# Side by side in the first expert too: its values and residuals from the fifth step on

## The chip, the cores and the metric

The kernel runs on one core of one Trainium2 chip. The metric is the device time in microseconds; lower is better. A core has five engines with a program each: TensorE for matmuls (PE in the profile, with its weight loads as PEld), VectorE (DVE), ScalarE (ACT), GpSimd (POOL) and SyncE (SP), which here issues most of the DMAs.

## The reference

The output is a gated mix of two parts for 2048 tokens of width 448: a Fourier mix of the tokens (part a) and a mixture of 8 experts (part b), in which each token goes to the two experts with the largest gate.

```python
gates = _softmax(xt @ wg, axis=-1)
topk_idx = jnp.argsort(-gates, -1)[:, :K]              # K = 2 of E = 8
...
h = _gelu(jnp.einsum("nd,edf->nef", xt, w1))           # 448 -> 1792
y = jnp.einsum("nef,efd->ned", h, w2)                  # 1792 -> 448
out = jnp.einsum("ne,ned->nd", cw, y)
...
return g * a + (1 - g) * b
```

The change touches the first product of one expert, `x @ w1` with the gelu behind it.

## The kernel before

**Stages.** The first 36 us hold the Fourier part's hidden transform, its quarter-length sequence transform and the gate logits. Then come the 8 experts, which the kernel orders by how many tokens they drew. Expert 0 (the fullest) has room for 552 tokens, experts 1 to 3 for 544, 528 and 528, experts 4 to 7 for 496 (`CAPS`). Each expert takes `NF` = 14 steps, one for each 128 of the 1792 hidden units, so there are 112 steps; below, step u of expert 0 is its step number, 0 to 13, and step 14 is the first of expert 1.

**One step.** `up(u)` forms 128 hidden units for all tokens of the expert in PSUM, and `down(u)` multiplies the result with 128 rows of `w2` into five PSUM banks that collect over the 14 steps. To keep precision, every operand is a rounded value and the residual that the rounding left: `hi` and `lo` of the weights, and in the tile `X[e]` four chunks of 128 features of rounded tokens (index 0 to 3) and three of residuals (4 to 6; the residual of the short fourth chunk sits in that chunk's free rows). A product is the sum of value times value, value times residual, and residual times value.

The tokens of a step are worked in two parts (`hf` 0 and 1), as a PSUM bank (the tile `acc`, three buffers) takes 512 columns of 4 bytes. In expert 0 the parts are 276 and 276 columns. Each part is 11 matmuls into one `acc`: `hi` with three value chunks, `hi` with three residual chunks, `hi` with the fourth chunk, `lo` with four value chunks. Then ScalarE applies the gelu from PSUM to the tile `g` (L794).

In experts 1 to 3 `pairs(e)` is true: the first part is 256 columns, and one matmul of 512 columns streams a value chunk and its residual chunk side by side, into the two halves of the bank. That part is 8 matmuls, and its sum has to be finished: ScalarE copies the residual half from PSUM to `g` (L792), VectorE adds the value half to it (L793), and then ScalarE applies the gelu to `g` in place (L794).

After both parts, `g` is rounded to `gh`, by ScalarE in experts 1 to 3 and in steps 4 to 13 of expert 0 (L805), else by VectorE (L807), and VectorE forms the residual `gl` (L811) and some small pieces (L818, L819). `down(u)` needs `gh` and `gl`.

**Order.** The order of instructions on TensorE, VectorE, ScalarE and SyncE is that of the program text. The loop over u issues: `turn_due` (a tile of gathered tokens of the next expert is split into values, L695 on ScalarE, and residuals, L696 and L697 on VectorE); `prep(u + 2)` (the weights of the step after next are rounded on ScalarE, L226, and their residuals formed on VectorE, L231, after which SyncE fetches further weights); while u < 11 `advance(2)`, the next pieces of the routing work; `stage` (VectorE transposes a gathered tile, `blocks`, L684, and GpSimd gathers another, L675); `up(u + 1)`; `down(u)`; and `side_work`, a check of the transform matrices on VectorE. In experts 1 to 3 the side work is issued between the two parts of `up`, in expert 0 behind `down`; it begins at u = 11.

**Routing work in expert 0.** The routing generator makes the token lists and weights on VectorE with long instructions: `oa` (L394), `ob` and `vtok` (L398, L402), `piece` (L420, 16 short ones), `part` and `vw` (L426 to L433), then the place tables. TensorE multiplies in between (L407 into `acc`, whose result gives `tok`, from L410; L438 into `acc`, whose result gives `wgt`, from L441). GpSimd gathers the tokens of expert 1 by `piece` from step 6 on, in five tiles of up to 128 tokens, with two buffers for gathered tiles (`xg`).

Of the kernel before, what the change touches and what calls it, by code (L numbers as in the profile page):

```python
# [20 lines left out]
P = 128  # L21
# [5 lines left out]
E = 8  # L27
F = 1792
NF = F // P
CAPS = (552, 544, 528, 528, 496, 496, 496, 496)  # L30
CMAX = 576
FULL = 4
# [33 lines left out]
def r32(ap):  # L66
    return ap.bitcast(F32)
# [7 lines left out]
def tile_kernel(ctx: ExitStack, tc: tile.TileContext, xt, xrows, xplain, wg, whid, cq, cw, cspec, edge, refs, wquad, whall, cgen, wcat, out):  # L75
# [103 lines left out]
    def clear(i):  # L179
        if i == 0:  # L180
            rt["zero"] = mp.tile([P, D], F32, name="yt", bufs=2)
            ve.memset(rt["zero"], 0.0)
        if i < NT + NCT:
            sp.dma_start(out[i * P : (i + 1) * P, :], rt["zero"])
# [9 lines left out]
    jobs = [(e, f) for e in range(E) for f in range(NF)]  # L194
# [18 lines left out]
    def extra(e):  # L213
        return max(0, CAPS[e] - FULL * P)

    def apart(e):
        return 0 < extra(e) <= Q
# [19 lines left out]
    def prep(k):  # L237
        if k < len(jobs):
            upper(k)
            lower(k)  # L240
# [250 lines left out]
    def advance(n=1):  # L491
        for _ in range(n):
            next(route, None)
# [205 lines left out]
    def turn0(c, n):  # L699
        if c == 0:  # L700
            X[0] = xp.tile([P, 2 * NC - 1, CMAX], F32R, name="X")
        pt = (psy if c > 1 else ps).tile([P, NC, P], F32, name=f"y{c - 2}" if c > 1 else "acc")
        xg = XG.pop(c)
        for k in range(NC):
            te.transpose(pt[:, k, :n], xg[:n, k * P : (k + 1) * P], ident[:n, :n])
        sl = slice(c * P, c * P + n)
        se.activation(X[0][:, :NC, sl], pt[:, :, :n], AF.Copy)
        TU[c] = pt, sl, n
# [3 lines left out]
    def left0(c):  # L712
        pt, sl, n = TU.pop(c)
        ve.tensor_tensor(X[0][:, NC:, sl], pt[:, : NC - 1, :n], r32(X[0][:, : NC - 1, sl]), OP.subtract)
        ve.tensor_tensor(X[0][64:P, NC - 1, sl], pt[64:P, NC - 1, :n], r32(X[0][64:P, NC - 1, sl]), OP.subtract)
# [5 lines left out]
    def turn_due(e, step, lag, pace):  # L721
        c = due(e, step - lag - 1, pace)
        if c is not None:
            turn(e, c)

    def stage(e, step, lag, pace):
        c = due(e, step - lag, pace)
        if c is not None:
            blocks(e, c)
        c = due(e, step, pace)  # L730
        if c is not None:
            gather(e, c)
# [24 lines left out]
    UP, GH, Y, REST = 0, {}, {}, {}  # L757
    last = len(jobs) - 1

    def pairs(e):  # L760
        return e > 0 and CAPS[e] > FULL * P

    def up(u, between=lambda: None):
        e, f = jobs[u]
        hi, lo = W[u]
        cap = CAPS[e]
        rem = extra(e)
        span = FULL * P if broad(u) else cap
        g = mp.tile([P, CMAX], F32, name="g")
        nh = 1 if cap <= 512 else 2  # L770
        cut = 2 * P if u == 0 or pairs(e) else cap // nh
        for hf in range(nh):
            cs = slice(hf * cut, cap if hf == nh - 1 else cut)
            xs = slice(cs.start, span if hf == nh - 1 else cut)
            n = cs.stop - cs.start
            acc = ps.tile([P, 512], F32, name="acc")
            part = lambda w, x, c: (w[:, c * P : (c + 1) * P], X[e][:, x + c, xs], xs.stop - xs.start)
            both = pairs(e) and hf == 0
            if both:
                steps = [(hi[:, c * P : (c + 1) * P], X[e][:, c : c + NC + 1 : NC, cs], 2 * n) for c in range(NC - 1)]  # L780
            else:
                steps = [part(hi, 0, c) for c in range(NC - 1)] + [part(hi, NC, c) for c in range(NC - 1)]
            steps += [part(hi, 0, NC - 1)] + [part(lo, 0, c) for c in range(NC)]
            if u == 0 and hf == 1:
                steps = steps[: NC - 1] + steps[2 * NC - 1 : -1] + steps[NC - 1 : 2 * NC - 1] + steps[-1:]
            for s, (a, b, m) in enumerate(steps):
                te.matmul(acc[:, :m], a, b, start=s == 0, stop=s == len(steps) - 1)  # L787
                if u == hf == 0 and s in (2, 5):
                    turn0(s // 3 + 3, tl0[s // 3 + 3])
                    left0(s // 3 + 3)  # L790
            if both:
                se.activation(g[:, cs], acc[:, n : 2 * n], AF.Copy)  # L792
                ve.tensor_tensor(g[:, cs], acc[:, :n], g[:, cs], OP.add)  # L793
            se.activation(g[:, cs], g[:, cs] if both else acc[:, :n], AF.Gelu_apprx_tanh)  # L794
            if hf == 0:
                between()
        if u == last:
            gh, gl = (stream.tile([P, DX], F32R, name=n) for n in ("hi", "lo"))
        else:
            gh = mp.tile([P, CMAX + RMAX], F32R, name="gh", bufs=3)  # L800
            gl = mp.tile([P, FULL * P], F32R, name="gl", bufs=3)
        main = cap - rem
        top = main if apart(e) else cap
        if pairs(e) or snug(e) and e < E - 1 or e == 0 and f >= 4:
            se.activation(gh[:, :top], g[:, :top], AF.Copy)  # L805
        else:
            ve.tensor_copy(gh[:, :top], g[:, :top])  # L807
        GH[u] = (gh, gl)

        def rests():  # L810
            ve.tensor_tensor(gl[:, :main], g[:, :main], r32(gh[:, :main]), OP.subtract)  # L811
            if apart(e):
                if f in LOTS:
                    rt["rest"] = mp.tile([P, NF, Q], F32, name="rest", bufs=2)
                REST[u] = rt["rest"][:, f - max(b for b in LOTS if b <= f)]
                ve.tensor_copy(REST[u][:, :rem], g[:, main:cap])
            elif rem:
                ve.memset(r32(gh[:, cap : main + RMAX]), 0.0)  # L818
                ve.tensor_tensor(gh[:, main + RMAX : main + RMAX + rem], g[:, main:cap], r32(gh[:, main:cap]), OP.subtract)  # L819

        if f == 0 and e > 0:
            return rests
        rests()

    def snug(e):
        return CAPS[e] == FULL * P - 16

    def broad(u):
        e, f = jobs[u]
        return snug(e) and (f < 2 and not snug(e - 1) or f == NF // 2 - 1 and e == E - 2)  # L830
# [266 lines left out]
    def side_work(s):  # L1097
# [27 lines left out]
        if s > end + 1 and 1 <= f < (NF - 3 if e == E - 1 else NF - 1) and len(summed) < NT:  # L1125
            mix(len(summed))

    up(UP, lambda: advance(2))
    def jump_hint():
        PE = mybir.EngineType.PE  # L1130
        tc.mark_branch_hint_location("rare", "LikelyTaken", [PE])
        mark = next(i for i in reversed(nc.cur_bb.bb.instructions) if i.engine == PE)
        tc.keep_in_program_order(SimpleNamespace(ins=mark))

    for u in range(UP, last):
        e, f = jobs[u]
        plan = (e + 1, f - 1, 2, 2) if e else (1, f - 6, 2, 1)
        turn_due(*plan)
        prep(u + 2)
        if u < UP + SIDE:  # L1140
            advance(2)
            clear(2 * (u - UP))
            clear(2 * (u - UP) + 1)
        if u == last - NF - 1:
            tc.keep_in_program_order(gp.drain())
        if u == UP + SIDE:
            for _ in route:
                pass
            ck = late.enter_context(tc.tile_pool(name="ck", bufs=2, side="right"))
        stage(*plan)  # L1150
        split = pairs(jobs[u + 1][0])
        if u + 3 == last:
            jump_hint()
        rests = up(u + 1, lambda: side_work(u - UP) if split else None)
        if u < last - 3:
            down(u, behind=rests)
        if not split:
            side_work(u - UP)
# [66 lines left out]
    with tc.For_i(0, n_a) as j:  # L1225
# [3 lines left out]
        for h in range(2):  # L1229
            hf = full.tile([P, 2 * D], F32, name="hf")  # L1230
# [133 lines left out]
```

## Time and profile before

| | |
|---|---|
| median of 3 runs | 620.47 us (620.4 to 620.85) |
| the profiled execution, its own time | 620.74 us |
| its span in the profile | 619.1 us |
| TensorE busy | 611.8 us, 99% of the span |
| VectorE busy | 482.8 us, 78% |
| ScalarE busy | 321.1 us, 52% |
| mean granted clock of TensorE | 0.997 |

The span runs from the first to the last instruction of the profiled execution; 1.6 us of its time lie outside. Busy times of matmuls are modelled, so the spacing of their starts says more than their durations.

### The profile page before, as it was taken

The page shows a single profiled execution, that of the slowest core. Times are in us where ns is not written, and L with a number is a line of the kernel's source. Part 1 is how long each engine was busy: PE and PEld are TensorE (multiplying, and loading weights), DVE is VectorE, ACT ScalarE, POOL GpSimd, SP SyncE. Part 2 cuts the span into 40 slices and gives each one's busy share as a digit, 9 for nine tenths or more (in the row PEclk, how much of TensorE's full clock was granted, in tenths as well). Part 3 has the DMA queues.
Part 4 walks back from the last instruction along what each step waited for, and adds up shares of the span by engine and source line. Part 5 has one row for each costly group of instructions (what it writes and reads, how often), then busy time and mean ns, then how long its engine had stood idle before and what let it go on. Part 6 is the DMA issues. An engine that isn't in the chain of part 4 may idle for free. (4 is left out here: it accounts for less than half of the span.)

```text
span 619.1 us, 10867 instructions
## 1 busy us (share of the span) xinstructions
PE 611.8 (99%) x3581; PEld 547.6 (88%) x3581; DVE 482.8 (78%) x1234; ACT 321.1 (52%) x642; POOL 219.8 (36%) x200
## 2 busy tenths in 40 slices
PE   9999999999999999999999999999999999999996
PEld 6999999999998999989999788888888888888885
DVE  8889688579978889879896698787995677566652
ACT  2553344566565566655565645554454545654440
POOL 2210075635154262444460445333350442142123
PEclk9999999999999999999999999999999999999998
DMA  8556455597667777777776868779576736768743
GB/s 345 188 160 216 158 190 166 145 257 236 214 226 190 207 239 235 237 190 209 242 235 224 200 201 264 237 208 285 191 241 195 154 117 146 158 149 181 148 84 76
DMA packets 58653, 122.94 MB, mean 199 GB/s; under 512 B 8356, under 2 KB 31740, under 8 KB 58592
## 3 DMA queue, kind: packets, MB, share of 16 engines
q1 hardware_dynamic: 47376, 101.95, 50.4%
q0 software_dynamic: 11072, 20.19, 17.5%
q8 instruction: 29, 0.48, 0.3%
q14 instruction: 32, 0.26, 0.1%
q10 hardware_dynamic: 144, 0.07, 0.0%
HBM read 106.27 MB, written 15.90 MB: 197 GB/s over the span
## 5 line engine op out<-in xcount | busy, mean ns | idle before, releaser
L861 PE MATMUL y<-ud,gh 128*128 128x448 f32 (+3 forms) x916 | 258.6, 363 | 0.0
L787 PE MATMUL acc<-X,hi 128*128 128x496 f32 (+5 forms) x1050 | 211.1, 337 | 0.0
L675 POOL DMA_INDIRECT xg<-xrows,piece x115 | 129.5, 1126 | 199.7 <-DVE xq L684 125.8
L787 PEld LDWEIGHTS acc<-X,hi 128*128 128x128 f32 x1050 | 171.8, 188 | 18.0 <-issue 1.1
L861 PEld LDWEIGHTS y<-ud,gh 128*128 128x128 f32 (+1 forms) x916 | 166.5, 185 | 12.7
L861 PE MATMUL y<-ud,gl 128*128 128x448 f32 (+1 forms) x444 | 162.3, 365 | 0.0
L794 ACT ACTIVATE g<-acc 128x496 f32<-128x496 f32 (+4 forms) x126 | 60.6, 481 | 166.1 <-PE acc L787 148.9
L787 PE MATMUL acc<-X,lo 128*128 128x496 f32 (+5 forms) x672 | 132.5, 319 | 0.0
L811 DVE TENSOR_TENSOR gl<-g,gh 128x512 fp32r<-128x512 f32 (+1 forms) x111 | 75.5, 680 | 62.8 <-ACT gh L805 61.5
L787 PEld LDWEIGHTS acc<-X,lo 128*128 128x128 f32 x672 | 104.8, 188 | 9.0
L926 POOL DMA_INDIRECT out<-ys,tok x36 | 64.3, 1787 | 109.4 <-DVE ys L916 35.1
L861 PEld LDWEIGHTS y<-ud,gl 128*128 128x128 f32 (+1 forms) x444 | 82.6, 186 | 11.7 <-DVE gl L811 0.2
L967 DVE CUSTOM_DVE_ANT_0 junk<-quads 128x512 f32<-128x512 f32 x128 | 87.8, 686 | 2.3
L231 DVE TENSOR_TENSOR lo<-raw,hi 128x512 fp32r<-128x512 f32 x112 | 77.0, 688 | 3.5 <-ACT hi L226 2.5
L226 ACT ACTIVATE hi<-raw 128x512 fp32r<-128x512 f32 x112 | 69.1, 617 | 0.0
L231 DVE TENSOR_TENSOR ud<-row,ud 128x448 fp32r<-128x448 f32 x112 | 69.1, 617 | 0.0
L226 ACT ACTIVATE ud<-row 128x448 fp32r<-128x448 f32 x112 | 63.1, 563 | 0.0
L805 ACT ACTIVATE gh<-g 128x512 fp32r<-128x512 f32 (+2 forms) x94 | 59.2, 630 | 3.0
L792 ACT ACTIVATE g<-acc 128x256 f32<-128x256 f32 x42 | 16.1, 382 | 42.9 <-PE acc L787 42.6
L794 ACT ACTIVATE g<-g 128x256 f32<-128x256 f32 x42 | 17.6, 418 | 39.4 <-DVE g L793 39.4
L1091 POOL DMA_DIRECT2D out<-ot x16 | 14.1, 904 | 57.0 <-ACT ot L1090 47.1
L793 DVE TENSOR_TENSOR g<-acc,g 128x256 f32<-128x256 f32 x42 | 17.3, 412 | 12.4 <-ACT g L792 12.4
(272 smaller groups left out, 386.0 us busy)
## 6 DMA issues: line engine op xcount, KB each, us to landing
quads<-cq SPq DMA_DIRECT2D x64, 512.0 KB, 5.2
raw<-wcat SPq DMA_DIRECT2D x112, 256.0 KB, 2.9
row<-wcat SPq DMA_DIRECT2D x112, 224.0 KB, 3.3
out<-yt SPq DMA_DIRECT2D x21, 224.0 KB, 3.3
xraw<-xt SPq DMA_DIRECT2D x8, 512.0 KB, 6.5
out<-ot POOLq DMA_DIRECT2D x16, 224.0 KB, 3.7
cw<-cw SPq DMA_DIRECT2D x4, 512.0 KB, 9.9
xg<-xrows,piece POOLq DMA_INDIRECT x115, 3.8
```

Source lines behind the costliest of these rows:

```text
L226: se.activation(hi[:, : raw.shape[-1]], raw, AF.Copy)
L231: ve.tensor_tensor(lo[:, :n], raw, r32(hi[:, :n]), OP.subtract)
L675: st = gp.indirect_dma_start(out=xg[:, q], out_offset=None, in_=xrows, in_offset=bass.IndirectOffsetOnAxis(ap=rt["piece"][:, e, g : g + 1] ...
L787: te.matmul(acc[:, :m], a, b, start=s == 0, stop=s == len(steps) - 1)
L792: se.activation(g[:, cs], acc[:, n : 2 * n], AF.Copy)
L793: ve.tensor_tensor(g[:, cs], acc[:, :n], g[:, cs], OP.add)
L794: se.activation(g[:, cs], g[:, cs] if both else acc[:, :n], AF.Gelu_apprx_tanh)
L805: se.activation(gh[:, :top], g[:, :top], AF.Copy)
L811: ve.tensor_tensor(gl[:, :main], g[:, :main], r32(gh[:, :main]), OP.subtract)
L861: te.matmul(Y[c][:m, o], a, b, start=f == 0 and s == 0, stop=f == NF - 1 and s == len(steps) - 1)
L926: st = gp.indirect_dma_start(out=out, out_offset=bass.IndirectOffsetOnAxis(ap=rt["tok"][:n, e, c : c + 1], axis=0), in_=ys[:n], in_offset= ...
L967: ve.tensor_tensor_reduce(out=junk[:, :512], in0=row(a[0])[:, a[1] * 512 : a[1] * 512 + 512], in1=row(b[0])[:, b[1] * 512 : b[1] * 512 + 5 ...
```

## The change

`pairs` gets the step as a second argument and becomes true for expert 0 from step 4 on as well. In these ten steps the first part of `up` is 256 columns with 8 matmuls (three of 512 columns, five of 256), followed by ScalarE's copy, VectorE's add and the gelu in place; the second part is 296 columns with 11 matmuls. Who rounds `g` to `gh` stays as it was, and the place of the side work too. Nothing else differs.

```diff
-    def pairs(e):
-        return e > 0 and CAPS[e] > FULL * P
+    def pairs(e, f=NF):
+        return CAPS[e] > FULL * P and (e > 0 or f >= 4)
...
-        cut = 2 * P if u == 0 or pairs(e) else cap // nh
+        cut = 2 * P if u == 0 or pairs(e, f) else cap // nh
...
-            both = pairs(e) and hf == 0
+            both = pairs(e, f) and hf == 0
...
-        if pairs(e) or snug(e) and e < E - 1 or e == 0 and f >= 4:
+        if pairs(e, f) or snug(e) and e < E - 1:
...
-        split = pairs(jobs[u + 1][0])
+        split = pairs(*jobs[u + 1]) and jobs[u + 1][0] > 0
```

## Rows read from the trace of the kernel before

**Rows 1.** The head of the page: the span, and each engine's busy time, share and instructions.

```profile
span 619.1 us, 10867 instructions
...
PE 611.8 (99%) x3581; PEld 547.6 (88%) x3581; DVE 482.8 (78%) x1234; ACT 321.1 (52%) x642; POOL 219.8 (36%) x200
```

**Rows 2.** The timeline of TensorE in expert 0 and the first two steps of expert 1; columns: start in us, us, engine, line, operation, out<-in, shape, count. In step 4 the first part begins at 56.87, the second at 58.26, `down` at 59.65. Then the two list products, the second part of step 12, both parts of step 14, and step 15.

```profile
56.87 1.04 PE L787 MATMUL acc<-X,hi 128*128 128x276 f32 x7
...
58.26 1.04 PE L787 MATMUL acc<-X,hi 128*128 128x276 f32 x7
...
59.65 0.57 PE L861 MATMUL y<-ud,gh 128*128 128x448 f32 x2
...
68.14 0.98 PE L407 MATMUL acc<-vtok,oa 128*128 128x40 f16 x32
...
91.61 1.86 PE L438 MATMUL acc<-vw,oa 128*128 128x120 bf16 x32
...
106.02 1.04 PE L787 MATMUL acc<-X,hi 128*128 128x276 f32 x7
...
115.90 0.98 PE L787 MATMUL acc<-X,hi 128*128 128x512 f32 x4
...
117.19 1.09 PE L787 MATMUL acc<-X,hi 128*128 128x288 f32 x7
...
121.52 0.97 PE L787 MATMUL acc<-X,hi 128*128 128x512 f32 x4
...
122.80 1.09 PE L787 MATMUL acc<-X,hi 128*128 128x288 f32 x7
...
124.26 0.56 PE L861 MATMUL y<-ud,gh 128*128 128x448 f32 x2
```

**Rows 3.** The timeline of VectorE, 56 to 118 us; in brackets the idle time before the instruction and what ended it. The rows of L811 are `gl` of steps 4 to 13.

```profile
58.04 2.35 DVE L394 TENSOR_TENSOR oa<-sr,one 128x1024 bf16<-128x1024 bf16 x2
60.98 0.69 DVE L811 TENSOR_TENSOR gl<-g,gh 128x512 fp32r<-128x512 f32 x1 [0.59 <-ACT gh L805]
...
66.61 0.69 DVE L811 TENSOR_TENSOR gl<-g,gh 128x512 fp32r<-128x512 f32 x1 [0.75 <-ACT gh L805]
...
69.16 0.20 DVE L410 TENSOR_SCALAR none<-acc 128x40 f32<-128x40 f32 x1 [0.60 <-PE acc L407]
...
73.19 0.69 DVE L811 TENSOR_TENSOR gl<-g,gh 128x512 fp32r<-128x512 f32 x1 [3.14 <-ACT gh L805]
...
78.82 0.69 DVE L811 TENSOR_TENSOR gl<-g,gh 128x512 fp32r<-128x512 f32 x1 [0.33 <-ACT gh L805]
...
84.46 0.69 DVE L811 TENSOR_TENSOR gl<-g,gh 128x512 fp32r<-128x512 f32 x1
...
86.32 1.48 DVE L433 TENSOR_TENSOR vw<-ob,part 128x1280 bf16<-128x1280 f32 x1
...
90.09 0.69 DVE L811 TENSOR_TENSOR gl<-g,gh 128x512 fp32r<-128x512 f32 x1 [1.66 <-ACT gh L805]
...
93.51 0.20 DVE L441 COPY wgt<-acc 128x40 f32<-128x40 f32 x1 [0.58 <-PE acc L438]
...
97.47 0.69 DVE L811 TENSOR_TENSOR gl<-g,gh 128x512 fp32r<-128x512 f32 x1 [1.47 <-ACT gh L805]
...
103.69 0.65 DVE L811 TENSOR_TENSOR gl<-g,gh 128x512 fp32r<-128x512 f32 x1
...
108.74 0.69 DVE L811 TENSOR_TENSOR gl<-g,gh 128x512 fp32r<-128x512 f32 x1 [0.30 <-ACT gh L805]
...
114.37 0.69 DVE L811 TENSOR_TENSOR gl<-g,gh 128x512 fp32r<-128x512 f32 x1 [2.57 <-ACT gh L805]
...
115.10 0.25 DVE L696 TENSOR_TENSOR X<-xq,X 128x96 fp32r<-128x96 f32 x1
...
117.81 0.42 DVE L793 TENSOR_TENSOR g<-acc,g 128x256 f32<-128x256 f32 x1 [0.97 <-ACT g L792]
```

**Rows 4.** The timeline of VectorE in step 15 (expert 1), around the add of the first part.

```profile
125.03 0.62 DVE L231 TENSOR_TENSOR ud<-row,ud 128x448 fp32r<-128x448 f32 x1
125.56 0.42 DVE L793 TENSOR_TENSOR g<-acc,g 128x256 f32<-128x256 f32 x1
127.43 0.69 DVE L811 TENSOR_TENSOR gl<-g,gh 128x512 fp32r<-128x512 f32 x1 [1.45 <-ACT gh L805]
```

**Rows 5.** The timeline of ScalarE: `gh` of step 4 in expert 0, then in step 15 the gelus of both parts and `gh`.

```profile
60.28 0.67 ACT L805 ACTIVATE gh<-g 128x552 fp32r<-128x552 f32 x1
...
126.02 0.42 ACT L794 ACTIVATE g<-g 128x256 f32<-128x256 f32 x1 [0.75 <-DVE g L793]
126.34 0.39 ACT L794 ACTIVATE g<-acc 128x288 f32<-128x288 f32 x1
126.77 0.63 ACT L805 ACTIVATE gh<-g 128x512 fp32r<-128x512 f32 x1
```

**Rows 6.** The timeline of GpSimd: the first and the last of the four gathers of the fourth tile of expert 1.

```profile
96.28 0.94 POOL L675 DMA_INDIRECT xg<-xrows,piece  x1 [0.56 <-DVE xq L684]
...
100.91 0.95 POOL L675 DMA_INDIRECT xg<-xrows,piece  x1 [0.30 <-issue]
```

**Rows 7.** The page's list of DMA issues: the gathers, with the median us from issue to landing.

```profile
xg<-xrows,piece POOLq DMA_INDIRECT x115, 3.8
```

**Rows 8.** Busy time by engine in a window, with the granted clock of TensorE, the DMA share and GB/s: expert 0 from step 4 on.

```profile
57.00:116.00 59.00, 59.00 (x426) 55.95 (x425) 45.64 (x122) 26.99 (x55) 25.89 (x23) 1.00 0.51 167
```

## The prediction

> **What bounds the kernel now.** The page's head comes first: TensorE is busy for 99% of the span, VectorE for 78%, ScalarE for 52% [rows 1]. So time can change in two ways only: TensorE gets less to do, or something makes it wait. The window of expert 0 from step 4 on says the same of the place of the change: TensorE is busy in all of its 59 us, at a granted clock of 1.00, which is the 2.4 GHz level, and VectorE for 45.6 us of them [rows 8]. The reader should then leave the shares and go to the two timelines of that stretch. On TensorE's, `up` of step 4 is two parts of 1.39 us, 56.87 to 58.26 to 59.65 [rows 2]. On VectorE's, the brackets are what matters: how long it idled before each `gl`, for that is all the room in which it can take more work before it falls behind [rows 3].
>
> **What is removed.** Ten steps lose three matmuls each, 22 become 19. The columns stay: 22 x 276 = 6072, against 3 x 512 + 5 x 256 + 11 x 296 = 6072. Does a matmul cost by its count or by its columns? Step 4 takes 2.78 us for 6072 columns in 22 matmuls, 0.458 ns a column; step 15, which is already paired, takes 2.74 us for 3 x 512 + 5 x 256 + 11 x 288 = 5984 columns in 19 matmuls, also 0.458 ns [rows 2]. So nothing worth counting is saved. By the limits of reading (0.01 us a boundary) ten steps hold 0.2 us at most; I take 0.
>
> The Trainium skill speaks for the change here. "TensorE: Matmul & The Clock Gate", section "Back-to-back issue gap", gives a sustained spacing of some 81 ns for 128 columns and 131 ns for 512, with weight loads and matmuls together. An estimate on the line between these two makes a pair cheaper than two single matmuls: about 100 ns for 276 columns, 103 for 296, 98 for 256, so 2.2 us a step before and 2.0 after, 1.9 us less over ten steps. The measured step is 2.78 us and does not lie on that line, so the trace disagrees.
>
> **What is added.** Each of the ten steps gets a copy of 256 columns on ScalarE and an add of 0.42 us on VectorE, and its first gelu reads `g`, behind the add. Ten adds are 4.2 us, and VectorE's brackets before `gl` and behind the two list products are 0.59 us before step 4's `gl` and 11.4 us after it, up to step 13 [rows 3]. By busy time the add fits. By order it may not: VectorE's queue is the program's, and in it the add of step u stands behind the weights' residuals, the routing pieces and the transpose, and directly ahead of `gl(u)`. Nothing stands between these two in expert 0. So from the add on, VectorE has nothing to run until ScalarE has done the first gelu, the second, and `gh`. Before, the first gelu needed only TensorE and was done while VectorE was still at the routing work.
>
> **The price of one late add.** If VectorE comes to the add later than the data (which are there 1.91 us into `up`, 115.90 to 117.81 in step 14 [rows 2, 3]), the chain starts with VectorE. Step 15 shows such a case: the instruction before ends at 125.65 (125.03 + 0.62), the add starts at 125.56, the first gelu at 126.02, the second at 126.34, `gh` at 126.77, `gl` at 127.43 [rows 4, 5]. That is 1.87 us from start to start, 1.78 us from the end of the instruction before. In expert 0 `gh` has 552 columns and took 0.67 us where step 15's took 0.63 [rows 5], and the second gelu has 8 columns more: 0.05 us together. So a late add puts **1.83 us** behind the end of VectorE's earlier work, or 1.92 where I count that work by starts.
>
> **Is it late in each step, and what does that add up to?** VectorE's own work from one `gl` to the next is the distance less the brackets, from rows 3: for steps 4 to 12 it is 4.88, 2.84 (less 0.60 and 3.14), 5.30, 5.64, 3.97, 5.33 (less 0.58 and 1.47), 6.22, 4.75 and 3.06, together 41.99 us. Step 4's add stands behind the two `oa`, which end at 60.39 (58.04 + 2.35); its data are there at 56.87 + 1.91 = 58.78. So it is late, and `gl` of step 4 starts at 60.39 + 1.83 = 62.22 instead of 60.98. From there each `gl` is the one before plus that step's work plus 1.83 (1.92 for the two steps without a bracket): 68.93, 73.60, 80.73, 88.29, 94.09, 101.25, 109.39, 115.97 and, for step 13, **120.86**, where it was 114.37. In each step the data of the add are there before VectorE, the tightest being step 6 with about 1 us, so the assumption holds throughout. VectorE is 6.5 us late by then.
>
> **Where TensorE meets it.** There is slack at first: `acc` has three buffers, and `gl(u)` is used only behind `up(u + 1)`. The list product at 68.14 needs `vtok`, done at 62.22 + 4.88 = 67.10; the one at 91.61 needs the last `vw`, which ended 3.34 us behind `gl` of step 8 (84.46; 86.32 + 1.48), now at 91.63: both nearly free. The first true wait is in step 12, whose second part reuses the buffer that the add of step 11 must have read. That add starts 1.92 us ahead of its `gl`, at 107.47, and ends at 107.9; TensorE came there at 106.02 [rows 2]: about 1.9 us. Smaller waits for `gl` and for the next buffer follow in steps 12 and 13.
>
> The last one sets the sum. Behind `gl` of step 13 VectorE forms the residuals of the fifth token tile of expert 1, and the second part of step 14 reads them from its fourth matmul on. They ended 0.98 us behind `gl` (114.37; 115.10 + 0.25), so now at 121.84. TensorE came to that matmul at 117.19 + 3 x 0.13 = 117.59. The wait moves it by 121.84 - 117.59 = **4.25 us**, with all earlier waits contained in it. Past it VectorE has room: in step 14 it waited 0.97 us before its add and again for `down`'s results, and step 13's `gl` is needed only behind `up` of step 14. So the delay stays at 4.25 us, and nothing later takes it back, since TensorE is the bound.
>
> The other costs lie under cover. The ten copies of ScalarE run where it waited for TensorE. The gathers of expert 1 start as much later as `piece`; four of them take 5.6 us to issue (96.28 to 100.91 + 0.95) and 3.8 us to land [rows 6, 7], 9.4 us, and with two buffers each has two VectorE rounds, over 14 us. If that cover were gone, the transposes would be later by what is missing. SyncE's fetches follow the weights' residuals, three steps ahead of their use.
>
> Sum: span 619.1 + 4.25 = 623.35; with the 1.6 us outside the span, 625.0 for the profiled execution's like. That execution (620.74) lies 0.27 above the median, 620.47, so the median after is **624.7**.
>
> **The rivals.**
> *Absorbed, the same time (chance 0.09).* The delay is what is left of ten chains: `gl` of step 13 may start up to 116.6 before TensorE waits for the tile. With 60.39 + 41.99 + 10 times the chain, that asks for a chain of 1.42 us instead of 1.83 to 1.92. For it: ScalarE overlaps independent work, and 0.3 to 0.4 us of each chain is the second gelu. Against: step 15's rows, where that overlap is already in. It gives 620.5 (at most 0.2 us less).
>
> *Faster (0.05).* If dropping a weight load and a matmul saves a whole slot of 2.78 / 22 = 0.126 us, 30 of them are 3.8 us, 616.7, as long as VectorE keeps up. For it: weight loads are busy 56 of 59 us in this stretch [rows 8]. Against: the equal 0.458 ns a column. The point that decides is the first part's time, 1.28 us in step 15 [rows 2] where columns alone give 2816 x 0.458 = 1.29. The skill's line above is a milder form of it, 618.6.
>
> *Slower still (0.11).* If TensorE's waits let its clock fall to the 1.2 GHz level, the matmuls behind them take twice as long, so each us at that level costs half a us more; or the wait for the fifth tile holds the whole second part of step 14 (0.4 us); or VectorE's lag meets the scatter of expert 0. From 626.2 up. No row of this stretch has a wait of TensorE, so the clock stays open.
>
> **How the numbers follow.** The forecast itself, 0.75: the chain is bounded by 1.65 us (the second gelu's start hidden) and 2.0 us (every instruction with its full length), ten times -0.2 and +0.15 us, so its own range is 622.7 to 626.2. For eight in ten I reach down towards the absorbed case and up into the slower one, 621.7 to 626.8; the absorbed, the faster and the rest of the slower case are left out, 2 in 10. A measurement of this kernel tells about 0.2%, 1.2 us, from no change. Faster 0.05, same 0.09, slower 0.86.
>
> **What would show it.** Right: the first parts of steps 4 to 13 take 1.28 us and the second 1.50; VectorE's add has no wait before it; `gl` waits some 1.4 us for `gh` in every step; idle time of TensorE appears from step 8 to 14, most at the second parts of steps 12 to 14, and in sum some 4 us; step 15 on is as before, only later. Wrong: adds that wait for ScalarE's copy (VectorE is not late), a first part clearly under 1.28 us, or TensorE waits in experts 1 to 3 that were not there.

## The result and the profile after

The changed kernel takes 624.83 us (median of 6 runs, 624.71 to 625.18) where the kernel before takes 620.4 (median of 6); the ratio is 1.0072, with a 95% interval of 1.0061 to 1.0084. It is slower by 4.4 us, and the prediction said 624.7. The profiled execution took 624.74 us, with a span of 623.1 us and a mean granted clock of 0.998.

The page's head after, beside [rows 1]: TensorE's busy time grew by 2 us while it has 30 instructions less, so busy time alone would mislead.

```profile
span 623.1 us, 10828 instructions
...
PE 613.7 (98%) x3551; PEld 546.5 (88%) x3551; DVE 486.2 (78%) x1244; ACT 322.9 (52%) x652; POOL 218.1 (35%) x200
```

The timeline of VectorE after, the rows that answer to [rows 3]: the end of `oa`, then the add and `gl` of steps 4, 5, 8 and 11, the transpose of step 12, the add and `gl` of step 13, and the fifth tile's residuals.

```profile
58.05 2.36 DVE L394 TENSOR_TENSOR oa<-sr,one 128x1024 bf16<-128x1024 bf16 x2
60.32 0.42 DVE L793 TENSOR_TENSOR g<-acc,g 128x256 f32<-128x256 f32 x1
62.22 0.69 DVE L811 TENSOR_TENSOR gl<-g,gh 128x512 fp32r<-128x512 f32 x1 [1.49 <-ACT gh L805]
...
67.02 0.41 DVE L793 TENSOR_TENSOR g<-acc,g 128x256 f32<-128x256 f32 x1
68.92 0.69 DVE L811 TENSOR_TENSOR gl<-g,gh 128x512 fp32r<-128x512 f32 x1 [1.48 <-ACT gh L805]
...
86.38 0.42 DVE L793 TENSOR_TENSOR g<-acc,g 128x256 f32<-128x256 f32 x1
88.28 0.69 DVE L811 TENSOR_TENSOR gl<-g,gh 128x512 fp32r<-128x512 f32 x1 [1.49 <-ACT gh L805]
...
107.25 0.38 DVE L793 TENSOR_TENSOR g<-acc,g 128x256 f32<-128x256 f32 x1
109.12 0.69 DVE L811 TENSOR_TENSOR gl<-g,gh 128x512 fp32r<-128x512 f32 x1 [1.49 <-ACT gh L805]
...
113.45 0.71 DVE L684 STREAM_TRANSPOSE xq<-xg 128x512 f32<-128x512 f32 x1 [0.35 <-issue]
...
118.94 0.39 DVE L793 TENSOR_TENSOR g<-acc,g 128x256 f32<-128x256 f32 x1
120.82 0.69 DVE L811 TENSOR_TENSOR gl<-g,gh 128x512 fp32r<-128x512 f32 x1 [1.49 <-ACT gh L805]
...
121.55 0.25 DVE L696 TENSOR_TENSOR X<-xq,X 128x96 fp32r<-128x96 f32 x1
```

None of the ten adds has a bracket: each starts as soon as VectorE gets to it. Every `gl` has the same one, 1.48 or 1.49 us, in which VectorE stands still for ScalarE, where [rows 3] has brackets from none to 3.14 us, set by TensorE's pace. The lateness of `gl` against [rows 3] is 1.24 us in step 4 and 6.45 us in step 13.

The timeline of ScalarE in step 8 shows why, and answers to [rows 5]: the copy is done by 82.33, and then ScalarE waits 4.50 us for the add, with the second part's gelu and `gh` queued behind.

```profile
81.95 0.38 ACT L792 ACTIVATE g<-acc 128x256 f32<-128x256 f32 x1 [0.26 <-PE acc L787]
86.83 0.42 ACT L794 ACTIVATE g<-g 128x256 f32<-128x256 f32 x1 [4.50 <-DVE g L793]
87.16 0.40 ACT L794 ACTIVATE g<-acc 128x296 f32<-128x296 f32 x1
87.59 0.67 ACT L805 ACTIVATE gh<-g 128x552 fp32r<-128x552 f32 x1
```

The timeline of TensorE after, beside [rows 2]: step 4, whose first part now takes 56.88 to 58.17, then the second parts of steps 12, 13 and 14 (the last in two rows), and step 15.

```profile
56.88 0.98 PE L787 MATMUL acc<-X,hi 128*128 128x512 f32 x4
...
58.17 1.12 PE L787 MATMUL acc<-X,hi 128*128 128x296 f32 x7
...
59.67 0.57 PE L861 MATMUL y<-ud,gh 128*128 128x448 f32 x2
...
107.69 1.22 PE L787 MATMUL acc<-X,hi 128*128 128x296 f32 x7 [1.41 <-DVE g L793]
...
114.53 1.22 PE L787 MATMUL acc<-X,hi 128*128 128x296 f32 x7 [0.65 <-DVE g L793]
...
121.03 0.67 PE L787 MATMUL acc<-X,hi 128*128 128x288 f32 x3 [0.34 <-ACT X L695]
121.85 0.80 PE L787 MATMUL acc<-X,hi 128*128 128x288 f32 x4 [0.15 <-DVE X L696]
...
125.85 0.98 PE L787 MATMUL acc<-X,hi 128*128 128x512 f32 x4
```

TensorE waits for the add that has to free a buffer (steps 12 and 13), then for the fifth token tile of expert 1: first for its values, which ScalarE makes behind `gh` of step 13 (L695), then for its residuals (L696). The brackets of the matmuls sum to 2.6 us. Those of the weight loads (PEld) from 104 to 124 us sum to 4.2 us, in six places; two of the six are waits for `gl`, in steps 12 and 13, which the matmul rows don't show:

```profile
109.86 0.19 PEld L861 LDWEIGHTS y<-ud,gl 128*128 128x128 f32 x1 [0.38 <-DVE gl L811]
...
116.70 0.19 PEld L861 LDWEIGHTS y<-ud,gl 128*128 128x128 f32 x1 [0.38 <-DVE gl L811]
```

By starts, step 12's second part is 1.67 us late, step 15 is 4.33 us late (125.85 against 121.52), and it is 4.34 us in the last expert too (its last matmul starts at 617.23 against 612.89). Nothing is given back on TensorE. The span grew by 4.0 us only, as the tail behind the last matmul came out 0.3 us shorter.

### The profile page after: what moved, and what is told of

It is laid out like the page before. It is cut to its first block, busy times and chain, and to the rows that moved or that the text cites. A ratio compares the mean times of both kernels' runs of the same rounds, so it can differ in the third digit from the quotient of the medians.

```text
span 623.1 us, 10828 instructions
## 1 busy us (share of the span) xinstructions
PE 613.7 (98%) x3551; PEld 546.5 (88%) x3551; DVE 486.2 (78%) x1244; ACT 322.9 (52%) x652; POOL 218.1 (35%) x200
## 5 line engine op out<-in xcount | busy, mean ns | idle before, releaser
L787 PE MATMUL acc<-X,hi 128*128 128x496 f32 (+6 forms) x1020 | 211.8, 343 | 2.6 <-DVE g L793 2.1
L787 PEld LDWEIGHTS acc<-X,hi 128*128 128x128 f32 x1020 | 169.8, 188 | 22.2 <-DVE g L793 2.5
L787 PE MATMUL acc<-X,lo 128*128 128x256 f32 (+6 forms) x672 | 132.6, 319 | 0.0
L811 DVE TENSOR_TENSOR gl<-g,gh 128x512 fp32r<-128x512 f32 (+1 forms) x111 | 75.6, 681 | 66.9 <-ACT gh L805 65.7
L794 ACT ACTIVATE g<-acc 128x496 f32<-128x496 f32 (+5 forms) x116 | 56.5, 487 | 134.0 <-PE acc L787 119.7
L794 ACT ACTIVATE g<-g 128x256 f32<-128x256 f32 x52 | 21.8, 418 | 71.3 <-DVE g L793 71.3
L792 ACT ACTIVATE g<-acc 128x256 f32<-128x256 f32 x52 | 19.7, 379 | 47.2 <-PE acc L787 44.0
L793 DVE TENSOR_TENSOR g<-acc,g 128x256 f32<-128x256 f32 x52 | 21.4, 411 | 11.3 <-ACT g L792 11.2
```

## The experiments

Two theories stood against each other. Mine: the cost is the place of VectorE's add in its queue, ten late chains through ScalarE. The rival: pairing itself costs, by its matmul shapes or by ScalarE's copy.

**The chain without the pairing.** The kernel before, with a copy and a VectorE instruction that changes no value put between the first part and its gelu:

```diff
+            chained = e == 0 and f >= 4 and hf == 0
+            if chained:
+                se.activation(g[:, cs], acc[:, :n], AF.Copy)
+                ve.tensor_tensor(g[:, cs], acc[:, :n], g[:, cs], OP.max)
-            se.activation(g[:, cs], g[:, cs] if both else acc[:, :n], AF.Gelu_apprx_tanh)
+            se.activation(g[:, cs], g[:, cs] if both or chained else acc[:, :n], AF.Gelu_apprx_tanh)
```

> The kernel before, with no pairing (276 and 276 columns, 22 matmuls), but in steps 4 to 13 of expert 0 the first part's gelu is put behind a copy by ScalarE and one VectorE instruction of 276 columns, which takes the larger of two equal values and so changes no number. Theory (the place of VectorE's instruction in its queue costs the time, ten late chains of 1.83 to 1.92 us): about as slow as the changed kernel, 4.0 to 4.5 us over the kernel before, gl of step 13 at about 120.9. Rival (the pairing itself costs: other matmul shapes, two streams out of one tile): within 0.5 us of the kernel before.

Measured: 625.35 us against 620.96 for the kernel before on the same chip (chips differ a little, so each run goes beside the kernel before on its own), ratio 1.0072 (1.0055 to 1.0089), the same ratio as that of the whole change. VectorE's timeline in step 13: `gl` at 121.12, with the same bracket (expected about 120.9).

```profile
119.22 0.41 DVE L797 TENSOR_TENSOR g<-acc,g 128x276 f32<-128x276 f32 x1
121.12 0.69 DVE L815 TENSOR_TENSOR gl<-g,gh 128x512 fp32r<-128x512 f32 x1 [1.49 <-ACT gh L809]
```

The loss comes back in full without a single changed matmul.

**The pairing without the add.** The first gelu reads the bank's value half; ScalarE's copy stays:

```diff
-                ve.tensor_tensor(g[:, cs], acc[:, :n], g[:, cs], OP.add)
-            se.activation(g[:, cs], g[:, cs] if both else acc[:, :n], AF.Gelu_apprx_tanh)
+                if e:
+                    ve.tensor_tensor(g[:, cs], acc[:, :n], g[:, cs], OP.add)
+            se.activation(g[:, cs], g[:, cs] if both and e else acc[:, :n], AF.Gelu_apprx_tanh)
```

> The changed kernel without VectorE's add in expert 0: the first gelu reads the value half of the bank, and ScalarE's copy stays. So the products with the tokens' residuals are left out for the first 256 tokens of steps 4 to 13. Theory: nothing waits for VectorE, gl of step 13 is back near 114.4 and the time within 0.5 us of the kernel before. Rival (the matmul shapes, or ScalarE's copy, cost the time): 4 us over the kernel before, as the changed kernel.

Measured: 621.14 against 620.96 us, ratio 1.0004 (0.9995 to 1.0014). `gl` of step 13 is at 114.84 and waits for TensorE's pace again, 2.60 us. The rival's 4 us are far outside: the matmul shapes and the copy cost nothing that the times can tell from noise (the interval reaches from 0.3 us faster to 0.9 us slower), and they gain nothing either.

```profile
114.84 0.69 DVE L812 TENSOR_TENSOR gl<-g,gh 128x512 fp32r<-128x512 f32 x1 [2.60 <-ACT gh L806]
```

**The same work in another order.** The changed kernel, with the routing pieces and the transposes of these steps issued behind the add, between the two parts (`lists` holds what the loop did at once before; `filled` is true where `up(u + 1)` is one of steps 4 to 13):

```diff
-        stage(*plan)
+        if not filled:
+            stage(*plan)
+        def work():
+            if split:
+                side_work(u - UP)
+            if filled:
+                lists()
+                stage(*plan)
...
-        rests = up(u + 1, lambda: side_work(u - UP) if split else None)
+        rests = up(u + 1, work)
```

> The changed kernel with the routing pieces, the zeroing of rows and the transposes of steps 4 to 13 issued behind the add, between the two parts of up, as experts 1 to 3 do with their side work. Theory: the work now runs in the 1.4 us in which VectorE waited for gh, a step costs VectorE its own 3 to 6.3 us and 0.4 for the add, under TensorE's 5.67 on average, the lateness does not build up, and the time is within 0.6 us of the kernel before (no gain, since pairing saves nothing). Rival (matmul shapes or the copy cost, not the order on VectorE): still 4 us over. A second rival (VectorE simply has too little time for ten more adds, whatever the order): 2 us over or more.

Measured: 621.28 against 620.96 us, ratio 1.0008 (0.9998 to 1.0018). VectorE's timeline in step 7 and at the add of step 8:

```profile
76.90 0.42 DVE L793 TENSOR_TENSOR g<-acc,g 128x256 f32<-128x256 f32 x1 [1.48 <-ACT g L792]
77.24 3.43 DVE L420 TENSOR_SCALAR piece<-tf 32x40 int32<-32x40 f32 x16
80.70 0.69 DVE L811 TENSOR_TENSOR gl<-g,gh 128x512 fp32r<-128x512 f32 x1
...
82.56 0.42 DVE L793 TENSOR_TENSOR g<-acc,g 128x256 f32<-128x256 f32 x1
```

In step 7 the add now waits for its data, the long `piece` runs where VectorE stood still before, and `gl` follows with no bracket. The ten adds and all other work are there as in the changed kernel; only the order differs, on VectorE and, as the list products move along, on TensorE, and the loss is gone. So "VectorE has too little time for ten more adds" falls.

**Fewer steps.** Pairing from step 8, and from step 12 on (`gh` stays on ScalarE from step 4 in both):

```diff
-        return CAPS[e] > FULL * P and (e > 0 or f >= 4)
+        return CAPS[e] > FULL * P and (e > 0 or f >= 8)    # and 12
```

> Pairing from step 8 on, six steps instead of ten. Theory: by the same sum the add of step 8 starts behind the second vw, gl of step 8 starts at 86.4 and that of step 13 at 118.9, where 116.6 is free; so 2.3 us over the kernel before. Rival (every paired step costs the same, 4.3 / 10): 2.6 us over, with TensorE's steps longer one by one; the places of its waits tell the two apart: by the theory TensorE waits only in steps 12 to 14, by the rival in each step from 8 on.

Measured: 622.93 against 620.96 us, ratio 1.0034 (1.0021 to 1.0046), 2.1 us over. `gl` of step 13 is at 118.94 (expected 118.9). TensorE's waits in this stretch are these, in steps 13 and 14, and there is none from step 8 to 12:

```profile
112.65 1.22 PE L787 MATMUL acc<-X,hi 128*128 128x296 f32 x7 [0.32 <-DVE g L793]
...
119.16 0.66 PE L787 MATMUL acc<-X,hi 128*128 128x288 f32 x3 [0.34 <-ACT X L695]
119.98 0.80 PE L787 MATMUL acc<-X,hi 128*128 128x288 f32 x4 [0.16 <-DVE X L696]
```

By time the two accounts were too near (2.3 and 2.6); by the place of the waits it is the theory's, though the wait that it had in step 12 did not come.

> Pairing in steps 12 and 13 alone. Theory: gl of step 13 starts at 115.2, under the 116.6 that is free, so TensorE waits for nothing and the time is that of the kernel before within 0.4 us. Rival (each paired step costs 0.43 us): 0.9 us over.

Measured: 621.96 against 621.47 us, ratio 1.0008 (0.9998 to 1.0018), 0.5 us where at most 0.4 was expected and the interval holds no change; the rival's 0.9 us is inside its upper end (1.1 us) too, so by time alone this run doesn't decide. Its trace does. TensorE has no bracket from step 4 to the first steps of expert 1, and step 15 begins 64.71 us after step 4:

```profile
57.54 1.04 PE L787 MATMUL acc<-X,hi 128*128 128x276 f32 x7
...
122.25 0.97 PE L787 MATMUL acc<-X,hi 128*128 128x512 f32 x4
```

In the kernel before it is 64.65 us (56.87 to 121.52 [rows 2]). The stretch of the change is 0.06 us longer, where the rival asks for 0.9; the rest of what the medians differ by lies outside it or in the noise. Six steps cost half of what ten cost, and two nothing that is clear of noise: the bill is what is left of the chains past the slack.

**A chain twice as dear.** A second VectorE instruction behind each of the ten adds:

```diff
                 ve.tensor_tensor(g[:, cs], acc[:, :n], g[:, cs], OP.add)
+                if e == 0:
+                    ve.tensor_tensor(g[:, cs], g[:, cs], g[:, cs], OP.max)
```

> The changed kernel with a second VectorE instruction of 256 columns behind each of the ten adds (it takes the larger of two equal values and changes no number), so each chain is some 0.42 us longer. Theory: the ten chains stand in one row, so the delay grows by all ten of them, 4.2 us, to 8.5 us over the kernel before (628.9). Rival (the delay is a fixed wait, as for the gathers or for a buffer, or the added busy time counts only where VectorE is full): 0 to 2 us more than the changed kernel.

Measured: 629.93 against 621.47 us, ratio 1.0141 (1.0126 to 1.0157), 8.5 us by the medians and 8.8 by the ratio: twice the loss. TensorE's first wait now comes in step 9 (1.38 us), so the slack is used up earlier. Step 13:

```profile
123.23 0.39 DVE L793 TENSOR_TENSOR g<-acc,g 128x256 f32<-128x256 f32 x1
123.65 0.48 DVE L795 TENSOR_TENSOR g<-g 128x256 f32<-128x256 f32 x1
125.62 0.69 DVE L813 TENSOR_TENSOR gl<-g,gh 128x512 fp32r<-128x512 f32 x1 [1.49 <-issue]
```

From this trace's add of step 4 (60.50) to its `gl` of step 13 are 65.12 us, in the changed kernel 60.50 (60.32 to 120.82): 4.62 us more for ten instructions, 0.46 each, which is one instruction and its hand-over. VectorE sets the pace of these steps, and each addition to the chain counts in full.

**What pairing is worth at all.** The kernel before with no pairing in experts 1 to 3 either:

```diff
-        cut = 2 * P if u == 0 or pairs(e) else cap // nh
+        cut = 2 * P if u == 0 else cap // nh
...
-            both = pairs(e) and hf == 0
+            both = False
```

> The kernel before with no pairing anywhere: experts 1 to 3 work two even parts with 11 matmuls each (22 a step instead of 19), without the copy and the add (42 of each gone); gh stays on ScalarE and the side work between the parts. Theory (a matmul costs by its columns, and in experts 1 to 3 the side work fills VectorE's waits): within 0.5 us of the kernel before; three matmuls a step more at some 2.5 ns each would be 0.3 us. Rival (pairing is worth its weight loads where VectorE keeps up): 42 x 3 slots of about 0.12 us, 15 us slower, or a share of that.

Measured: 621.6 against 620.84 us, ratio 1.0013 (1.0004 to 1.0022). It is slower by 0.8 us (0.25 to 1.4), more than the 0.5 us expected: 42 steps, 0.02 us each on average. So where VectorE's waits are filled, pairing is worth a little; it is nowhere near a slot per matmul.

**The runs on one scale.** The times of the experiments come from three chips. The stretch of the change alone can be read in each trace, from the first matmul of step 4 to the first of step 15:

| run | step 4 to step 15, us | over the kernel before, us |
|---|---|---|
| the kernel before | 64.65 | |
| the changed kernel | 68.97 | 4.32 |
| the chain without the pairing | 69.21 | 4.56 |
| the pairing without the add | 64.89 | 0.24 |
| the same work in another order | 64.88 | 0.23 |
| pairing from step 8 | 66.74 | 2.09 |
| pairing in steps 12 and 13 | 64.71 | 0.06 |
| a chain twice as dear | 73.62 | 8.97 |

The loss lies in this stretch and goes with the late chains. Where the adds delay nothing, ten paired steps still take 0.24 us more on TensorE, some 0.02 us each.

## Why the prediction was right, step by step

**What is removed: right at the size of the reading error.** Step 4's first part takes 1.29 us and its second 1.50 (rows of TensorE above), 2.79 us in place of 2.78 [rows 2]. The 0.24 us that ten paired steps take more where the adds delay nothing (the table above) were put at 0; in the changed kernel they run in the time that TensorE loses at step 14 anyhow. The rival in which each dropped matmul saves a slot fails, and the run without the add shows it with no chain in the way. The line through the two spacings that the Trainium skill gives ("TensorE: Matmul & The Clock Gate", "Back-to-back issue gap") would put the first part at about 0.9 us, an estimate; the trace has 1.29 us, so the measurement decides against it.

**The price of a late add: right.** 1.90 us from start to start in step 4, 1.87 in step 11 where the add took 0.38; 1.92 was worked out from step 15, in expert 1. From the end of VectorE's earlier work it is 1.81 us in step 4 (60.41 to 62.22), against 1.83. The rival in which the delay is absorbed asked for 1.42.

**The sum of the chains: right, the last digits by luck.** `gl` was forecast at 62.22, 68.93, 88.29, 109.39 and 120.86 in steps 4, 5, 8, 11 and 13, and stands at 62.22, 68.92, 88.28, 109.12 and 120.82. Step 11 is 0.27 early: steps 9, 10 and 11 came out 0.03, 0.11 and 0.12 shorter than forecast, 0.03 of it in each chain, the rest in VectorE's work between the chains. (It isn't the way of counting by starts: step 8, counted so, fits to 0.01.) Step 12 came out 0.26 longer, as its transpose waited 0.35 us for something the profile doesn't show. That the two cancel is luck; either alone would have moved the result by some 0.3 us.

**Where TensorE meets it: right in the end, loose on the way.** The fourth matmul of step 14's second part was forecast for 121.84 and starts at 121.85. The wait in step 12 was forecast at about 1.9 us, and by starts it is 1.67, as the add of step 11 came 0.22 us earlier than forecast. The list of what would show it named idle time from step 8 on; there is none before step 12. The text above it had both list products as nearly free and the first true wait in step 12, and the list should have followed it. It also promised idle time of some 4 us in sum; the brackets of the matmuls hold 2.6 and those of the weight loads 4.2. In step 14 the forecast had one wait, at the fourth matmul; the first one waits too, for ScalarE's values, and that wait is contained in the other.

**What comes later: right.** The delay stays at 4.34 us to the last expert, and the granted clock of TensorE stays at its 2.4 GHz level through the waits: 1.00 from 106 to 123 us, so that part of the slower rival did not happen. The longest bracket there is 1.41 us; in the run with the chain twice as dear it is 1.91 us, and the granted clock is 1.00 there too (108 to 128 us). From 124 us on the profile lists the same waits for TensorE and its weight loads as in the kernel before, so VectorE's lag didn't meet the scatter of expert 0 either.

```profile
57.00:106.00 49.00, 49.00 (x337) 45.21 (x335) 37.51 (x99) 20.41 (x45) 17.88 (x16) 1.00 0.50 167
106.00:123.00 17.00, 14.44 (x80) 12.10 (x79) 11.87 (x35) 9.17 (x21) 7.68 (x8) 1.00 0.32 102
```

This is the busy time by engine in two windows after. In the first, TensorE is busy in all 49 us although VectorE is getting later: three buffers hide it. In the second it loses 2.6 us. VectorE is busy for 37.5 us of the first 49, less than in the same window before:

```profile
57.00:106.00 49.00, 49.00 (x364) 46.49 (x363) 38.72 (x102) 21.36 (x43) 20.12 (x17) 1.00 0.53 174
```

The engine that sets the pace shows free time on the page, 11.5 us of it in this window, and 10.4 of these are the brackets before the seven `gl`, which wait for ScalarE.

No version tried beats the kernel before. The reordered one removes the loss, but there is no gain under it.

## What to carry to other kernels

An instruction put between two others on different engines costs an in-order queue the whole way there and back, here 1.9 us for an add of 0.4, if that queue reaches it late and the next thing in it waits for the end of the chain; ask what else stands around it in program order, and issue the bulk work after it rather than ahead of it. Sum the chains over the steps and subtract the slack once, at the place where the next consumer reads: a few steps may be free and ten cost 4 us. And before matmuls are merged, divide the measured time of a part by its columns: if the quotient is the same with fewer, longer matmuls, as it was in the kernel before (0.458 ns in steps 4 and 15), there is little to be had.

## What the runs showed that was not expected

In expert 0 a paired step is not even slightly faster: 5.67 us (56.88 to the next step's 62.55) against 5.64 (56.87 to 62.51), with `down`, whose matmuls are the same, 0.02 us longer as well. In expert 1 an unpaired step of 272 and 272 columns takes 5.24 us (152.75 to 157.99) where the paired one takes 5.19 (152.63 to 157.82). In expert 3 it is 5.10 us (292.23 to 307.54, three steps) against 5.09 (291.60 to 306.86). These are hundredths with opposite signs at equal columns, and the runs don't say where they come from.
